# The first query and key projections of a four-layer kernel: paired 64-row matmuls, and a new order of loads, norms and output halves

## The chip, the cores and the metric

The kernel runs on one core of a Trainium2 chip. The metric is the device time of one execution in microseconds (us); the time before is 1153.98 us, the median of three runs (1153.71 to 1154.44).

## The reference

Four layers run in the order A, B, A, B on x of 2048 rows by 576 columns, each adding to x. Layer A is an attention over a dilated window:

```
qkv = layernorm(x) @ wqkv                 # 576 -> 3 * 576, 32 heads of 18
key of query s: s, s-2, ..., s-14         # 8 keys, those below 0 masked
x = x + softmax(q.k * 18**-0.5) v @ wo
```

Layer B is a gated MLP whose gate mixes over the rows:

```
z = gelu(layernorm(x) @ w_in)             # 576 -> 4608
g = w_sp @ layernorm(z[:, 2304:]) + b_sp  # over the 2048 rows
x = x + (z[:, :2304] * g) @ w_out
```

## The kernel before, in words

Nearly all of the time goes to layer B, whose matmuls run as pairs in 64-row halves of the array (`mm_phase`, L234): in a first phase output 0 takes the upper 64 rows and output 1 the lower 64, in a second phase they change places. A bank may take only one half at a time, so between the phases stands a token: a small ScalarE copy (`turn_on`) that waits for the end of the first phase and that the second phase waits for. The change concerns layer A, above all the first (li = 0), at the start of the program.

Layer A stores x with even rows first, then odd rows, so that a window is contiguous. The program order on every engine, SyncE's DMA queue (SP) among them, is the order of the code. The opening of layer 0 is written out by hand:

- The x tiles of 128 rows are loaded, `S_` takes their statistics on VectorE, `R_` their inverse deviation (GpSimd power, L728), `A_` normalizes them (L735). `T_pe` transposes tiles 0 to 3 on TensorE; `T_` (`ln_T`, L306) has the DMA transpose tiles 4 to 15 into `xnT`, from the SP queue.
- `VW(t, hh)` (L451) computes half of v of attention tile t, five matmuls 128x288, evicted to `v_ext`. Attention tile t covers 120 queries (the first 128), so VW(8) and VW(9) need normalized tile 8.
- `PG(d, qk, cc)` (L462) is a projection unit: 128 output columns (block d of 0 to 4) of q or k for the 512 rows of chunk cc, five matmuls of 128 contracted rows over 512 columns, the fifth (`wqk4`, columns 512 to 575) padded with zero rows. Its eviction (L445 on ScalarE, L443 on VectorE) goes to a staging tile `stg`. Once q and k of a block are complete for cc 0 and 1, eight DMAs, dealt to the POOL and SP queues, move the heads' rows into `QK`. Block 4 holds the rests of both q and k.
- The window's mask is 14 rows more of `QK` in each head's 32. They are built in `R` (rows[0] to rows[3]), written in 16-byte pieces to the DRAM tile `win_period` (rows[2]; its first columns by rows[3]), loaded back four times by `load_pat` into `win_pat`, and spread over `QK` by `fill_window_rows` (L201, L204) before the heads' rows are laid over them.

Before the change the order on TensorE is: `T_pe` with VW(0) to VW(3); 18 units, nine for cc = 0 and nine for cc = 1; VW(4) to VW(7); four units of cc = 2; the logits of step 0 (`L_mm`, L536); four more units of cc = 2; VW(8); then 34 steps. On SP: the loads, rows[2], the load of x tiles 12 to 15, `T_` of tiles 4 to 7, `load_pat`, `T_` of tiles 8 to 11, 17 DMAs to `QK`, `T_` of tiles 12 to 15.

Step s runs the logits of step s+1, their exponentials on ScalarE (L545), the product with v (`PV`, L559), and what a table adds: the remaining units (steps 0 to 9 for cc = 2 and 3), the remaining VW, halves of the output projection (`WO`, L629), and TensorE's transposes of attention output (`O_T`, L595) of the tiles in `pe_turn`. `units` says in which steps the 32 WO halves stand; those at 34 and later run behind the last step. The logits take three PSUM banks (X) and one of two (Y) in turn; the rest shares the other Y and three PT banks.

Of the kernel before, what the change touches and what calls it, by code (L numbers as in the profile page):

```python
# [12 lines left out]
f32 = mybir.dt.float32  # L13
# [50 lines left out]
class K:  # L64
# [53 lines left out]
    def build_window_rows(self, c, R):  # L118
# [30 lines left out]
        one = self.dram.tile([2, MR, 2 * P + 8], bf16, name="win_period")  # L149
        for xb in self.xn_bufs:  # L150
            nc.gpsimd.memset(xb[:, D:640], 0.0)

# [43 lines left out]

    def fill_window_rows(self, QK, half):
        nc, n = self.nc, self.cfg.S // 2
        for g0 in (0, 4):
            for a in range(2):  # L200
                nc.vector.tensor_copy(out=QK[:, a, g0:g0 + 4, half * n:(half + 1) * n].rearrange("p g (k x) -> p g k x", x=P),  # L201
                                      in_=self.pat[:, a, half, None, None, :].to_broadcast([P, 4, n // P, P]))
            if half == 0:
                nc.vector.tensor_copy(out=QK[:, :, g0:g0 + 4, 0:8], in_=self.pat0[:, :, None, :].to_broadcast([P, 2, 4, 8]))  # L204
# [132 lines left out]
    def zero_right(self, wqk=True):  # L337
# [4 lines left out]
        nc.vector.memset(R["wo"][64:128, 4, :], 0.0)  # L342

    def load_wqk(self, eng, twice=False):

        R = self.right
        for c0, n, w0 in ((D, 512, D + 64), (0, D, 0), (D + 512, 64, D)):
            self.dma(R["wqk"][:, :, w0:w0 + n], self.A_wqkv[0:512, c0:c0 + n].rearrange("(c p) n -> p c n", p=P), eng=eng)
            for r in ((0, 64) if twice else (0,)):
                self.dma(R["wqk4"][r:r + 64, w0:w0 + n], self.A_wqkv[512:576, c0:c0 + n], eng=eng)  # L350
# [30 lines left out]
    def layer_A(self, li):  # L381
# [206 lines left out]

        pe_turn = tuple(range(0, 6)) + tuple(range(7, NT - 2, 2)) + (NT - 3,) if li == 0 else ()

# [85 lines left out]
        if li == 0:  # L676
# [10 lines left out]
            x_load(x0[:, 0:1, :], 0, 1, nc.sync)  # L687
            x_load(x0[:, 1:2, :], 1, 1, nc.scalar)
            x_load(x0[:, 2:4, :], 2, 2, nc.sync)
            self.load_wv(nc.sync, 2)  # L690
# [3 lines left out]
            exp_table()  # L694
            self.zero_right()
            self.make_ident()
            warm = self.PT_tile([P, 512], f32, "warm")
            for _ in range(46):
# [3 lines left out]
                sb, oT[:].rearrange("p a b -> p (a b)")[:, 4 * D:4 * D + nR].rearrange("p (a r b m) -> p a r b m", a=2, r=MR, b=2))  # L702
            nc.scalar.copy(out=v_ext[:, :, :, DH:DH + 1], in_=self.ones[:, None, None, :].to_broadcast([P, NT, H, 1]))
            rows[0]()
# [26 lines left out]
            def A_(*tiles):  # L731
                for i in tiles:
                    xns[i] = xn = self.xn_bufs[self.xn_rr % len(self.xn_bufs)]
                    self.xn_rr += 1
                    nc.vector.tensor_scalar(out=xn[:, 0:D], in0=xts[i], scalar1=mvs[:, i, 0:1],  # L735
                                            scalar2=rstds[:, i:i + 1], op0=ALU.subtract, op1=ALU.mult)

            def T_pe(i):
# [8 lines left out]
            def T_(*tiles):  # L747
                for i in tiles:
                    self.ln_T(xns.pop(i), i * P, P)
# [10 lines left out]
            rows[2](nc.sync)  # L760
            A_(3)
            VW(2, 0, False)
            T_pe(3)
# [6 lines left out]
            S_(4, 5)  # L770
            R_(4, 2)
            A_(4, 5)
            T_(4, 5)
            S_(6, 7)
            R_(6, 2)
            rows[3](nc.gpsimd)
            A_(6, 7)
            T_(6, 7)
            S_(8)
            self.load_pat(nc.sync)  # L780
            S_(9, 10, 11)
            R_(8, 4)
            S_(12)
            A_(8, 9, 10, 11)
            T_(8, 9, 10, 11)
            self.fill_window_rows(QK, 0)
            S_(13, 14, 15)
            order = [(d, cc) for cc in range(2) for d in range(5)]
            for k_, (d, cc) in enumerate(order):
                for qk in ((1, 0) if d < 4 else (0,)):  # L790
                    PG(d, qk, cc, False, (nc.gpsimd, nc.sync) if d in (0, 3, 4) else q2)
                if k_ == 7:
                    R_(12, 4)
            nvw0, nvw = 4, 9
        else:
# [33 lines left out]
        def at(s, f, *a):  # L829
            table.setdefault(s, []).append((f, a))  # L830
# [10 lines left out]
        for k_, (d, qk, cc) in enumerate(pgs):  # L841
            at(k_ if li == 0 else (k_ * PG_END) // len(pgs), PG, d, qk, cc, True, *((q2,) if li == 0 else ()))
        vws = [(t, hh) for t in range(nvw, NT) for hh in range(2)]
        lag, twice = (PG_END - 5, (PG_END - 2,)) if li == 0 else (9, ())
        vsteps = ([x for x in range(PG_END - 4, NST - 3) if x % 4] if li == 0 else
                  [6, 6] + list(range(8, NST)))
        for k_, (t, hh) in enumerate(vws):
            assert vsteps[k_] <= 2 * t - 2 + hh
            at(vsteps[k_], VW, t, hh, (k_ % 2 == 0 or k_ > len(vws) - 4) if li == 0 else vsteps[k_] >= PG_END - 4 and k_ % 2 == 0)
        units = [x for x in range(lag, NST) for _ in range(2 if x in twice else 1)]  # L850
        units += [NST] * 3 + [NST + 1] * 2 + [NST + 2] * 2 if li > 0 else [NST] * 2 + [NST + 1] * 4
        wo_steps = list(zip(units[0::2], units[1::2]))
# [416 lines left out]
```

## Time and profile before

| what | value |
|---|---|
| profiled execution | 1153.91 us |
| its span, first to last instruction | 1152.1 us |
| mean granted TensorE clock | 1.000 |
| TensorE (matmul) busy | 1144.3 us, 12949 instructions |
| VectorE, ScalarE, GpSimd busy | 537.9, 371.8, 259.9 us |
| moved by DMA | 91.26 MB |

The span is cut by stage: the opening of layer 0 until about 48 us, its steps until 122 us, layer B until 581 us, the second layer A until 689 us, the second layer B until the end. A line of the timeline gives start, duration, engine, line, operation, out<-in and count, and in brackets the idle time before it and who ended it. A line of the chain of waits gives start, duration, engine, tile, line and count. "SPq" is the issuing of a DMA, not its transfer. Durations of matmuls in the timeline overlap; the chain's do not.

### The profile page before, as it was taken

What the parts mean: (1) busy time and instruction counts of PE and PEld (TensorE: products, weight loads), DVE (VectorE), ACT (ScalarE), POOL (GpSimd) and SP (SyncE); (2) the same over time, 40 slices, a digit from 0 to 9 for tenths busy, and PEclk for the clock granted to TensorE, in tenths of its full rate; (3) what the DMA queues carried; (4) which work ended last, traced back from release to release, by engine and by line L of the source; (5) the groups of instructions that cost most, each with busy time, mean ns of one, the idle gap of its engine ahead of it and who ended that gap; (6) DMA issues with size and microseconds to landing.
All of it is one profiled execution on the core that took longest, in us unless ns stands there. A gap on an engine that the chain in (4) does not pass through costs nothing.

```text
span 1152.1 us, 29708 instructions
## 1 busy us (share of the span) xinstructions
PE 1144.3 (99%) x12949; PEld 612.9 (53%) x12949; DVE 537.9 (47%) x1193; ACT 371.8 (32%) x665; POOL 259.9 (23%) x387
## 2 busy tenths in 40 slices
PE   9999999999999999999999999999999999999998
PEld 5567554444444444457755774544444444444676
DVE  8789887312233222234466889843322223222311
ACT  5589565011111111102247876641111111011000
POOL 3689654000000000002153767530000000000000
PEclk9999999999999999999999999999999999999999
DMA  8878597000000000049455777930000000000322
GB/s 194 182 166 197 135 201 152 13 13 13 13 1 13 13 13 2 1 143 221 109 111 112 172 161 167 227 83 1 13 13 13 13 13 1 13 1 28 103 74 58
DMA packets 177373, 91.26 MB, mean 79 GB/s; under 512 B 128788, under 2 KB 170420, under 8 KB 177242
## 3 DMA queue, kind: packets, MB, share of 16 engines
q1 hardware_dynamic: 164762, 70.75, 28.1%
q0 software_dynamic: 5888, 12.72, 4.5%
q10 hardware_dynamic: 6592, 5.90, 1.7%
q8 instruction: 101, 1.65, 0.6%
q14 instruction: 30, 0.25, 0.1%
HBM read 35.46 MB, written 14.69 MB: 44 GB/s over the span
## 4 chain that ended last, share of the span: by engine, by line
PE 97%; ACT 1%; DVE 1%; issue 1%; DVEq 0%; ACTq 0%
PE hh L234 79%; PE pp L462 6%; PE pv L451 3%; PE pw L629 3%; PE O_ps L559 2%; PE L_ps L536 2%; ACT P_sb L545 1%; PE L_ps L462 1%; PE hh L1191 0%; DVE ln_st L715 0%; PE pt L595 0%; DVE ln_xn L735 0%; ACT v_ext L445 0%; DVE win_bits L158 0%; ACT xnT L745 0%
## 5 line engine op out<-in xcount | busy, mean ns | idle before, releaser
L234 PE MATMUL hh<-Wq,Z 64*128 64x512 bf16 x4608 | 505.8, 376 | 0.0
L234 PEld LDWEIGHTS <-Z 64*128 64x128 bf16 x6984 | 338.3, 94 | 311.6
L1095 DVE TENSOR_TENSOR g_tmp<-hh,ln_xn 128x512 f32<-128x512 f32 x144 | 92.8, 686 | 452.3 <-PE hh L234 452.3
L947 ACT COPY bank_turn<-ones 1x1 bf16<-1x1 bf16 x239 | 44.7, 187 | 538.6 <-PE hh L234 538.6
L78 POOL DMA_DIRECT2D wout<-in_B_w_out_dram x4 | 4.3, 1075 | 602.0 <-PE hh L234 602.0
L234 PE MATMUL hh<-wout,Z 64*128 64x288 bf16 x2232 | 137.0, 283 | 0.0
L545 ACT ACTIVATE P_sb<-L_ps 128x1440 bf16<-128x1440 f32 (+3 forms) x136 | 125.1, 972 | 22.4 <-PE L_ps L536 21.1
L234 PE MATMUL hh<-xnT,w 64*128 64x512 bf16 x1152 | 132.1, 376 | 0.0
L234 PE MATMUL hh<-win2a,xnT 64*128 64x512 bf16 (+1 forms) x960 | 118.6, 355 | 0.0
L234 PEld LDWEIGHTS <-xnT 64*128 64x128 bf16 x1440 | 69.6, 94 | 70.3 <-issue 0.5
L1020 DVE BATCH_NORM_STATS2 z_st<-zp 128x6 f32<-128x512 bf16 (+1 forms) x160 | 92.6, 623 | 11.1 <-ACT zp L1018 11.1
L1086 ACT ACTIVATE z1T<-hh 128x1024 bf16<-128x1024 f32 x72 | 73.7, 1024 | 61.9 <-PE hh L234 61.9
L1096 DVE TENSOR_TENSOR Z<-g_tmp,z1T 128x512 bf16<-128x512 f32 x144 | 92.4, 683 | 0.0
L234 PEld LDWEIGHTS <-w 64*128 64x128 bf16 x1152 | 55.8, 94 | 68.5
L1018 ACT ACTIVATE zp<-hh 128x1024 bf16<-128x1024 f32 (+1 forms) x96 | 76.1, 810 | 48.8 <-PE hh L234 48.7
L462 PE MATMUL pp<-xnT,wqk_sb 128*128 128x512 bf16 (+1 forms) x330 | 75.5, 379 | 0.0
L234 PE MATMUL hh<-win2b,xnT 64*128 64x512 bf16 (+1 forms) x480 | 72.8, 355 | 0.0
L1160 DVE TENSOR_TENSOR x_new<-hh,xo 128x288 bf16<-128x288 f32 x64 | 26.3, 453 | 93.0 <-PE hh L234 89.3
L299 POOL TENSOR_SCALAR ln_xn<-x_new,ln_mv,ln_rstd 128x576 bf16<-128x576 bf16 x28 | 64.2, 2293 | 2.6
L78 POOL DMA_DIRECT2D QK<-stg x76 | 48.0, 635 | 36.2 <-DVE stg L443 22.0
L1044 POOL TENSOR_SCALAR Z<-zp,z_mv,z_rstd 128x256 bf16<-128x256 bf16 x32 | 51.2, 1599 | 3.5
L462 PEld LDWEIGHTS <-wqk_sb 128*128 128x128 bf16 (+1 forms) x360 | 32.1, 97 | 36.6 <-issue 2.3
(124 smaller groups left out, 754.1 us busy)
## 6 DMA issues: line engine op xcount, KB each, us to landing
xres<-x_new SPq DMA_DIRECT2D x44, 144.0 KB
wout<-in_B_w_out_dram POOLq DMA_DIRECT2D x4, 1296.0 KB, 7.6
xo<-xres SPq DMA_DIRECT2D x32, 144.0 KB
xn_rows<-ln_xn SPq DMA_DIRECT2D x28, 160.0 KB
w<-in_B_w_in_dram SPq DMA_DIRECT2D x16, 256.0 KB
QK<-stg POOLq DMA_DIRECT2D x51, 72.0 KB, 4.3
QK<-stg SPq DMA_DIRECT2D x37, 72.0 KB
xo<-in_A_x_dram SPq DMA_DIRECT2D x6, 288.0 KB
```

Of the source, the lines that this page charges most:

```text
L78: return eng.dma_start(out=out, in_=in_)
L234: ins = self.nc.tensor.matmul(outs[a_], lhsT=lhs(a_, c, r0), rhs=rhs(a_, c, r0), start=start and k_ == 0, stop=stop and k_ == len(chunks) ...
L299: e.tensor_scalar(out=xn[:nrows, 0:D], in0=x_t[:nrows, :], scalar1=mv[:nrows, 0:1], scalar2=rstd[:nrows, 0:1], op0=ALU.subtract, op1=ALU.mult)
L462: nc.tensor.matmul(pp, lhsT=w, rhs=self.xnT[r0:r1, c, cc * 512:(cc + 1) * 512], start=start, stop=stop, tile_position=(r0, 0))
L545: nc.scalar.activation(out=P_bufs[2 * jp + s % 2][:nk, :, :, 0:nq], in_=Lv[:nk, :, :, 0:nq], func=ACT.Exp, scale=scale)
L947: self.turn_on = lambda tok: nc.scalar.copy(out=tok, in_=self.ones[0:1, 0:1])
L1018: nc.scalar.activation(out=zp[:, w0:w0 + n], in_=pz, func=ACT.Gelu_apprx_tanh)
L1020: nc.vector.bn_stats(out=st[:, x // 512, :], in_=zp[:, x:x + min(512, w0 + n - x)])
L1044: eng.tensor_scalar(out=Z[:, b0:b1, i, :], in0=zv[:, b0:b1, :], scalar1=mv[:, 0:1], scalar2=rstd[:, 0:1], op0=ALU.subtract, op1=ALU.mult)
L1086: lambda ht, z1T=z1T, q2=q2: nc.scalar.activation(out=z1T[:, q2 * 512:(q2 + 2) * 512], in_=ht[:].rearrange("p a b -> p (a b)"), func=ACT.G ...
L1095: nc.vector.tensor_tensor(out=tmp[:], in0=pg[:, a_, :], in1=bsp[:, qs], op=ALU.add)
L1096: nc.vector.tensor_tensor(out=uT(jj)[:, sub, qs], in0=tmp[:], in1=z1Ts[jj, sub][:, qs], op=ALU.mult)
```

## The change

- The 18 units of cc 0 and 1 become nine pairs in 64-row halves (`PG_first` and its `second`), four chunks in the first phase, five in the second. The banks rotate over three pairs: two of X, the two of Y, two of PT. A pair's first phase stands ahead of the second phase of the pair before. The order is k and q of blocks 0 to 3 for cc = 0 (four pairs), then k with q of each block for cc = 1, then block 4. VW(4) stands around the second phase of the fourth pair, VW(5) around that of the last.
- `wqk4` and columns 576 to 639 of the normalized tiles hold the data of columns 512 to 575 twice, for tiles 0 to 7 by a GpSimd copy per tile, for the weights by three loads on the ScalarE queue (`load_wqk4_again`). The doubled weights are zeroed (VectorE) behind the last pair; the zeroing ahead of the opening and four GpSimd memsets go.
- rows[3] moves ahead, to the SP queue; `load_pat` moves from behind `T_` of tiles 6 and 7 to between `T_(4)` and `T_(5)`; the window fill is split in two among the norms. `T_` of tiles 8 and 9 stands behind the SP DMAs of block 0, that of tiles 10 and 11 behind those of block 1. `v_ext`'s ones are set by a GpSimd memset, not a ScalarE copy.
- VW(9) moves from steps 10 and 11 to ahead of the steps, and the VW behind it are dealt anew, so that steps 10 and 14 have none. VW evictions of the second layer A go to VectorE in other places. In both layers A one WO half moves from step 33 to step 32 (and in the second, halves at 34 to 36 to 33 to 35); tile 6 joins `pe_turn` in layer 0.

```diff
-        for xb in self.xn_bufs:
-            nc.gpsimd.memset(xb[:, D:640], 0.0)
...
+    def load_wqk4_again(self, eng):
+        for c0, n, w0 in self.WQK_PARTS:
+            self.dma(self.right["wqk4"][64:128, w0:w0 + n], self.A_wqkv[512:576, c0:c0 + n], eng=eng)
...
-        pe_turn = tuple(range(0, 6)) + tuple(range(7, NT - 2, 2)) + (NT - 3,) if li == 0 else ()
+        pe_turn = tuple(range(0, 7)) + tuple(range(7, NT - 2, 2)) + (NT - 3,) if li == 0 else ()
...
+            self.load_wqk4_again(nc.scalar)
...
-            self.zero_right()
+            self.zero_right(False)
...
-            nc.scalar.copy(out=v_ext[:, :, :, DH:DH + 1], in_=self.ones[:, None, None, :].to_broadcast([P, NT, H, 1]))
...
+                    if i < 8:
+                        nc.gpsimd.tensor_copy(out=xn[:, D:640], in_=xn[:, 512:D])
...
+            rows[3](nc.sync)
+            nc.gpsimd.memset(v_ext[:, :, :, DH:DH + 1], 1.0)
...
+            S_(6)
             A_(4, 5)
-            T_(4, 5)
-            S_(6, 7)
+            T_(4)
+            self.load_pat(nc.sync)
+            T_(5)
+            S_(7)
             R_(6, 2)
-            rows[3](nc.gpsimd)
+            S_(8)
             A_(6, 7)
             T_(6, 7)
-            S_(8)
-            self.load_pat(nc.sync)
+            self.fill_window_rows(QK, 0, (0,))
             S_(9, 10, 11)
             R_(8, 4)
             S_(12)
             A_(8, 9, 10, 11)
-            T_(8, 9, 10, 11)
-            self.fill_window_rows(QK, 0)
+            self.fill_window_rows(QK, 0, (4,))
             S_(13, 14, 15)
-            order = [(d, cc) for cc in range(2) for d in range(5)]
-            for k_, (d, cc) in enumerate(order):
-                for qk in ((1, 0) if d < 4 else (0,)):
-                    PG(d, qk, cc, False, (nc.gpsimd, nc.sync) if d in (0, 3, 4) else q2)
-                if k_ == 7:
-                    R_(12, 4)
-            nvw0, nvw = 4, 9
+            def PG_first(units, outs):
...
+                turn = self.mm_phase(outs, lhs, rhs, [0, 1, 2, 3], 0, True, False)
+                def second():
+                    self.mm_phase(outs, lhs, rhs, [0, 1, 2, 3, 4], 1, False, True, turn)
+                    for u, o in zip(units, outs):
+                        PG(*u, False, (nc.gpsimd, nc.sync) if u[0] in (0, 3, 4) else q2, pp=o)
+                return second
...
+            order = [((d, qk, 0), (d + 1, qk, 0)) for qk in (1, 0) for d in (0, 2)]
+            order += [((d, 1, 1), (d, 0, 1)) for d in range(4)] + [((4, 0, 0), (4, 0, 1))]
+            second = None
+            for p, units in enumerate(order):
+                if p == 4:
+                    self.ring = ["PT"]
+                    VW(4, 0, False)
+                    second()
+                    VW(4, 1, False)
+                    second = None
+                then = PG_first(units, pair_banks(p))
+                if second is not None:
+                    second()
+                    if p in (5, 6):
+                        T_(2 * p - 2, 2 * p - 1)
+                second = then
+            self.ring = ["Y", "Y", "PT", "PT", "PT"]
+            R_(12, 4)
+            VW(5, 0, True)
+            second()
+            nc.vector.memset(wqk4[64:128, :], 0.0)
+            VW(5, 1, False)
+            nvw0, nvw = 6, 10
...
-        lag, twice = (PG_END - 5, (PG_END - 2,)) if li == 0 else (9, ())
-        vsteps = ([x for x in range(PG_END - 4, NST - 3) if x % 4] if li == 0 else
+        lag, twice = (PG_END - 5, (PG_END - 2, NST - 2)) if li == 0 else (9, (NST - 2,))
+        vsteps = ([x for x in range(PG_END - 3, NST - 3) if x % 4 and x != PG_END] if li == 0 else
...
-            at(vsteps[k_], VW, t, hh, (k_ % 2 == 0 or k_ > len(vws) - 4) if li == 0 else vsteps[k_] >= PG_END - 4 and k_ % 2 == 0)
-        units = [x for x in range(lag, NST) for _ in range(2 if x in twice else 1)]
-        units += [NST] * 3 + [NST + 1] * 2 + [NST + 2] * 2 if li > 0 else [NST] * 2 + [NST + 1] * 4
+            at(vsteps[k_], VW, t, hh, k_ % 2 == 0 or (k_ > len(vws) - 4 if li == 0 else k_ < 6))
+        units = [x for x in range(lag, NST - 1) for _ in range(2 if x in twice else 1)]
+        units += [NST - 1] * (26 - len(units)) + [NST] * 2 + [NST + 1] * 4
```

More of the change, by code (lines that the diff above doesn't have):

```diff
@@ L195, in make_ident, with fill_window_rows @@
                                 base=0, pattern=[[-1, P]], channel_multiplier=1)
-    def fill_window_rows(self, QK, half):
+    def fill_window_rows(self, QK, half, g0s=(0, 4)):
         nc, n = self.nc, self.cfg.S // 2
-        for g0 in (0, 4):
+        for g0 in g0s:
             for a in range(2):
@@ L342, in zero_right @@
         nc.vector.memset(R["wo"][64:128, 4, :], 0.0)
+    WQK_PARTS = ((D, 512, D + 64), (0, D, 0), (D + 512, 64, D))
+    def load_wqk4_again(self, eng):
+        for c0, n, w0 in self.WQK_PARTS:
+            self.dma(self.right["wqk4"][64:128, w0:w0 + n], self.A_wqkv[512:576, c0:c0 + n], eng=eng)
     def load_wqk(self, eng, twice=False):
         R = self.right
-        for c0, n, w0 in ((D, 512, D + 64), (0, D, 0), (D + 512, 64, D)):
+        for c0, n, w0 in self.WQK_PARTS:
             self.dma(R["wqk"][:, :, w0:w0 + n], self.A_wqkv[0:512, c0:c0 + n].rearrange("(c p) n -> p c n", p=P), eng=eng)
@@ L794, in layer_A, with lhs, rhs @@
-            nvw0, nvw = 4, 9
+            self.turn_on = lambda tok: nc.scalar.copy(out=tok, in_=self.ones[0:1, 0:1])
+            def PG_first(units, outs):
+                def lhs(a_, c, r0):
+                    d, qk, cc = units[a_]
+                    w0 = d * P + (640 if qk else 0)
+                    return wqk[r0:r0 + 64, c, w0:w0 + P] if c < 4 else wqk4[r0:r0 + 64, w0:w0 + P]
+                def rhs(a_, c, r0):
+                    cc = units[a_][2]
+                    return self.xnT[r0:r0 + 64, c, cc * 512:(cc + 1) * 512]
+                turn = self.mm_phase(outs, lhs, rhs, [0, 1, 2, 3], 0, True, False)
[4 more added lines that the diff above has]
+                return second
@@ new lines, in pair_banks @@
+            def pair_banks(p):
+                if p % 3 == 0:
+                    return [X0[:, k_, :] for k_ in range(2)]
+                self.ring = [("Y", "PT")[p % 3 - 1]]
+                return [self.PT_tile([P, 512], f32, "pp")[:, :] for _ in range(2)]
+            order = [((d, qk, 0), (d + 1, qk, 0)) for qk in (1, 0) for d in (0, 2)]
[14 more added lines that the diff above has]
+                second = then
```

## The prediction

> **What bounds the kernel now.** I read the page's busy times first, then the chain of waits in order of time, then the timelines of the stages that the change touches.
>
> ```profile
> PE 1144.3 (99%) x12949; PEld 612.9 (53%) x12949; DVE 537.9 (47%) x1193; ACT 371.8 (32%) x665; POOL 259.9 (23%) x387
> PE 97%; ACT 1%; DVE 1%; issue 1%; DVEq 0%; ACTq 0%
> ...
> 13.61 19.47 PE pp L462 x90
> 33.08 4.90 PE pv L451 x40
> 37.98 4.32 PE pp L462 x20
> 42.79 4.42 PE pp L462 x20
> 47.21 1.23 PE pv L451 x10
> ```
>
> TensorE is busy for 99% and makes 97% of the chain. In the opening the chain is one unbroken row of matmuls from 13.61 to 48.44: 18 units in 19.47 (1.08 each), eight VW in 4.90 (0.61 each), four units of chunk 2, the first logits, four units, VW(8). So whatever shortens TensorE's work there counts, and so does any wait that opens there. Step 0 begins at 48.4. From the first chunk-2 unit to there it is 48.44 - 37.98 = 10.5 us, of which nothing changes.
>
> **TensorE's own work in the opening.**
>
> ```profile
> L234 PE MATMUL hh<-Wq,Z 64*128 64x512 bf16 x4608 | 505.8, 376 | 0.0
> ...
> 584.97 0.54 PE L_ps L462 x3
> 585.50 3.99 PE pp L462 x21
> 589.50 2.59 PE L_ps L462 x12
> ```
>
> Layer B's pairs do 4608 matmuls 64x512 in 505.8 us, 0.110 each, so two at a time take 0.220. A new pair needs 4 + 5 of these couples, 1.98 us, against 2.16 for two units: 0.18 saved, 1.7 over nine pairs. Against it: the array changes between 128-row and 64-row work. The second layer A shows that: from 584.97 to 589.50, 4.53 us, stand 8 half and 16 whole matmuls, worth 4 x 0.220 + 16 x 0.216 = 4.34; two changes cost 0.19, 0.1 each. The new opening has eight (into the pairs, in and out of each VW(4) half, in and out of VW(5), out at the end): 0.8. Net gain of the pairs: 0.9. Tokens and evictions (two of 0.59 and a copy per 1.98 us of ScalarE, a row below) stay hidden, since a second phase begins only behind the first phase of the next pair.
>
> VW(9) comes in addition, 1.2 us. Without any wait the first chunk-2 unit would begin at 37.98 - 0.9 + 1.2 = 38.3. VW(4) and VW(5) only change places.
>
> **The queue that feeds it.** Chunk cc = 1 needs tiles 4 to 7 transposed, chunk cc = 2 tiles 8 to 11; all of this goes through SP.
>
> ```profile
> 10.09 1.84 SPq L78 DMA_DIRECT2D win_period<-oT  x2
> 13.95 7.00 SPq L306 DMA_TRANSPOSE xnT<-ln_xn  x4
> 22.53 1.61 SPq L78 DMA_DIRECT2D win_pat<-win_period  x4
> 24.23 5.16 SPq L306 DMA_TRANSPOSE xnT<-ln_xn  x4
> 29.50 7.73 SPq L78 DMA_DIRECT2D QK<-stg  x9
> 37.33 6.41 SPq L78 DMA_DIRECT2D QK<-win2a  x8
> 43.85 5.19 SPq L306 DMA_TRANSPOSE xnT<-ln_xn  x4
> ...
> 17.91 0.76 POOL L78 DMA_DIRECT2D win_period<-win_first  x1 [0.31 <-POOL win_first L182]
> ...
> 25.42 2.36 DVE L201 COPY QK<-win_pat 128x4096 bf16<-128x4096 bf16 x2 [1.07 <-DMA win_pat<-win_period]
> ...
> 12.00:14.00 2.00, 1.81 (x14) 1.29 (x14) 1.12 (x5) 1.22 (x4) 0.70 (x1) 1.00 1.15 290
> 14.00:16.00 2.00, 2.00 (x11) 0.88 (x9) 1.92 (x7) 0.83 (x3) 0.00 (x0) 1.00 1.06 132
> 16.00:18.00 2.00, 2.00 (x11) 0.90 (x10) 1.17 (x4) 1.01 (x3) 1.36 (x6) 1.00 0.61 54
> 18.00:20.00 2.00, 2.00 (x11) 0.94 (x10) 1.93 (x8) 1.14 (x2) 0.66 (x1) 1.00 1.14 283
> ```
>
> Before, tiles 4 to 7 are issued by 20.95 and nine units from 13.61 reach cc = 1 at 23.35 without a pause: they landed within 2.4 us. `load_pat` stood behind them and waited until 22.53, 3.9 us after GpSimd's issue of rows[3] ended at 18.67. Now it stands ahead of T_(5), and all of SP waits with it for the period's 16-byte rows to land in DRAM.
>
> When do they land? They are issued at 10.09 to 11.93, but the windows show a queue that is full: 290 GB/s until 14, then 132 and 54 while the share of busy DMA stays at 1.06 and 0.61, then 283 again. A full queue that moves little is one of tiny pieces: I read the hole from 14 to 18 as these rows, behind the loads issued earlier. Floor: reached at 14 and landed 1.3 later (the lag of `load_pat` itself, issued until 24.14, used at 25.42), 15.3. Ceiling: the hole's end and 1.3, 19.3. The three extra weight loads (64 partitions x 1152 columns, 147 KB at 290 GB/s) push it 0.5 later. I take 18.1, near the end of the hole. Then four loads (1.61) end at 19.8, T_(5) to T_(7) (5.16 / 4 = 1.29 each) at 23.7, and land 1.4 later, at **25.1**; the lag is that of the plain load, and below the 2.4 of before.
>
> TensorE would want them at 13.61 + 4 pairs (7.9) + VW(4) (1.2) + five changes (0.5) = 23.2. It waits 1.9. This wait also swallows whatever moves ahead of it: the memset of the doubled weights and ScalarE's ones for `v_ext` that go, GpSimd's copy behind each normalized tile that comes.
>
> ```profile
> 1.10 0.54 DVE wqk_sb L340
> 2.59 2.54 ACT L703 COPY v_ext<-ones 128x544 bf16<-128x544 bf16 x1
> 17.00 0.78 DVE L735 TENSOR_SCALAR ln_xn<-x_in,lnx_mv,lnx_rstd 128x576 bf16<-128x576 bf16 x2 [0.81 <-POOL lnx_rstd L728]
> 28.74 9.79 POOL L78 DMA_DIRECT2D QK<-stg  x15 [5.88 <-ACT stg L445]
> 4.93 0.58 POOL L728 TENSOR_TENSOR lnx_rstd<-lnx_rstd,neg_half 128x1 f32<-128x1 f32 x1 [0.26 <-DVE lnx_rstd L727]
> 24.48 0.59 ACT L445 CAST stg<-pp 128x512 bf16<-128x512 f32 x1 [0.53 <-PE pp L462]
> ```
>
> They are worth from -0.5 (the memset's 0.54 off the start of VectorE's chain, if x has landed by then, which no row shows) to +0.6 (a GpSimd operation of 0.58 at most ahead of the first transposes); I take 0, as the 1.9 covers both ends. The `v_ext` memset on GpSimd lies between 0.1 and 2.5 us in its idle time; were VW evictions held by it, the same 1.9 covers that. On VectorE the norms of tiles 6 and 7 (17.00) come behind the statistics of tile 8, those of tiles 8 to 11 behind half the fill; SP asks for them at 21 and 32.5, with 3 us of room. On GpSimd the power for tiles 12 to 15 stands behind 19 DMAs, not 15 (0.65 each), so at about 29.2 + 12.4 = 41.6; SP gets to these tiles at 48.5.
>
> Second wait: T_ of tiles 8 to 11, formerly issued at 24.23 to 29.39 while SP had nothing else, now stand behind the DMAs of blocks 0 and 1. Block 0 is complete when the second phase of pair 4 is evicted: 25.1 + 0.9 + 0.9 + 1.1 + 1.2 (two evictions of 0.59) = 29.2. SP then issues four DMAs, T_(8, 9), three DMAs, T_(10, 11). A `QK` DMA takes (7.73 + 6.41) / 17 = 0.83: 29.2 + 7 x 0.83 + 4 x 1.29 = 40.2. Landing: between 1.3 (the plain load) and 4.3 (the page's median for `QK<-stg` from GpSimd, whose transfers share these DMA engines); I take 2.0, as the queue holds three such DMAs then, not the 17 it held before: **42.2**. TensorE would be there at 25.1 + 5 pairs (9.9) + VW(5) to VW(8) (4.9) + three changes (0.3) = 40.2. It waits 2.0 more.
>
> ```profile
> QK<-stg POOLq DMA_DIRECT2D x51, 72.0 KB, 4.3
> ```
>
> Step 0 so begins at 42.2 + 10.5 = 52.7 instead of 48.4: **+4.3**. The rest of the queue about keeps up: ten more DMAs end at 48.5, and were ready for the logits of step 1 before within 48.4 - 43.7 = 4.6, so by 49.9 to 53.1; tiles 12 to 15 are issued by 53.7, land by 55.7, and are wanted by the first cc = 3 unit at about 55.5. The window fill, moved ahead by `load_pat`, gains nothing: blocks 0 to 2 are later than the fill anyway.
>
> **The steps and the ends.**
>
> ```profile
> 69.28 0.39 PE L536 MATMUL L_ps<-QK 32*128 32x120 bf16 x16
> 71.73 0.39 PE L536 MATMUL L_ps<-QK 32*128 32x120 bf16 x16
> 78.29 0.39 PE L536 MATMUL L_ps<-QK 32*128 32x120 bf16 x16
> 80.35 0.39 PE L536 MATMUL L_ps<-QK 32*128 32x120 bf16 x16
> 90.98 3.74 ACT L545 ACTIVATE P_sb<-L_ps 128x1440 bf16<-128x1440 f32 x4
> 116.86 0.72 PE L559 MATMUL O_ps<-v_ext,P_sb 128*128 128x19 bf16 x16 [0.43 <-ACT P_sb L545]
> ...
> 627.20 0.39 PE L536 MATMUL L_ps<-QK 32*128 32x120 bf16 x16 [0.21 <-ACT P_sb L545]
> 683.42 0.72 PE L559 MATMUL O_ps<-v_ext,P_sb 128*128 128x19 bf16 x16
> ```
>
> Step 10 takes 71.73 - 69.28 = 2.45, step 14 80.35 - 78.29 = 2.06. Without their VW (0.6), and with a transpose more in step 14, TensorE needs about 1.85 and 1.7, but two exponentials take ScalarE 3.74, so no step is under 1.87: -0.6 and -0.2. At the end of layer 0 TensorE waits 0.43 for the last exponential (116.86); a WO half fills it: -0.4. In the second layer A the same wait is short (the transpose before ends about 683.2): -0.2, and the evictions off ScalarE take away the 0.21 at 627.20: -0.2. Sum -1.6. No row bounds the new places of these halves from above; a late row of `oT` would take back at most the 0.6.
>
> **Sum:** +4.3 - 1.6 = **+2.7**. The profiled execution took 1153.91 us (span 1152.1 and 1.8 around it; the median is 1153.98): **1156.6**.
>
> **A rule against it.**
>
> ```profile
> 6.03 0.45 PE L742 MATMUL pt<-ident,ln_xn 128*128 128x128 bf16 x5 [0.62 <-DVE ln_xn L735]
> ```
>
> The granted clock is 1.00 in every window above, and TensorE's wait of 0.62 at 6.03 lies ahead of them. The Trainium skill ("TensorE: Matmul & The Clock Gate", HAM oscillation) wants no idle gap over about 3.4 us, or the clock halves; no run here shows such a gap. My waits of 1.9 and 2.0 stay under it, and by the rule the sum stands unless either grows to that.
>
> **Rivals.**
> - *The order of SP alone decides.* The rows land by 16.2, tiles 4 to 7 by 23.2, and only the second wait is left: block 0 complete at 27.3, T_(11) issued at 38.3 and landed at 40.3. The opening is 40.3 - 38.0 = 2.3 longer, the sum +0.7, 1154.6. For it: the hole's first half; against: 54 GB/s until 18.
> - *Not slower: both transfers are hidden.* The place is SP's issue. If beside an emptier queue a `QK` DMA issues in 0.6 instead of 0.83, and tiles 4 to 7 land by 23.2, tiles 8 to 11 land by about 38.7: opening +0.7, total -0.9, 1153.0; with the changes of mode free (-0.8) and the memset's 0.5 in front, 1151.7 or less. It decides from a landing at 38.3. Against: 17 DMAs in a row at 0.83.
> - *The tail of the queue is late too.* With the lag of 4.3 behind tiles 12 to 15, they land at 58.0, wanted at 55.5: +2.5, 1159.1.
> - *The clock halves in a wait that grew.* After each wait as much work as it was long runs at half speed: +1.9 and +2.0, 1160.5.
> - *The pairs don't run two at a time.* Then a pair takes 3.9 us, +17 and more: 1172. Layer B's 0.110 speaks against it.
>
> **How the numbers follow.** Forecast 0.50, with 18.1 moved between 17.3 and 18.9 and the lag between 1.4 and 3: 1155.2 to 1158.4. SP alone 0.17, hidden 0.19, tail 0.09, clock 0.04, no overlap 0.01. A measurement of this kernel can tell 0.2%, 2.3 us, from no change: 1151.7 to 1156.3. The forecast is above it for 0.34 of its 0.50; with tail, clock and no overlap that is slower 0.48. Hidden is faster for 0.09 and same for 0.10; with SP alone and the forecast's 0.16 same is 0.43. The range from 1153.0 to 1159.4 takes in the forecast, SP alone, the tail and the slower half of hidden.
>
> **What would show it.** In the changed profile: the first `win_pat` load on SP at about 18; a pause of TensorE near 23 and 25, and one near 40 and 42, each ended by a DMA to `xnT`; pairs of 1.98 in between; step 0 near 52.7; steps 10 and 14 at 1.87. If `win_pat` goes out by 16, or the chain shows no pause there, the forecast is wrong, and the time lies nearer 1153.

## The result and the profile after

The changed kernel takes **1167.74 us** (median of five runs, 1165.06 to 1169.67) against 1153.98, a ratio of 1.0118 with a 95% interval from 1.0106 to 1.0129. The prediction was 1156.6 with a range to 1159.4: the sign was right, the size was not. The profiled execution took 1169.67, the slowest of the five; its span is 1167.9, 15.8 more than before.

From the page after: busy time by engine, the clock of TensorE in 40 slices of 29 us, and the chain by engine.

```profile
PE 1147.9 (98%) x13009; PEld 616.8 (53%) x13026; DVE 541.2 (46%) x1197; ACT 368.7 (32%) x669; POOL 262.3 (22%) x391
...
PEclk9799999999999999999999999999999999999999
...
PE 95%; DMA 1%; ACT 1%; DVE 1%; issue 1%; SPq 0%; POOL 0%; DVEq 0%; ACTq 0%
```

TensorE was busy 3.6 us longer for the same products, the second slice shows a clock of 0.7, and DMA now has 1% of the chain. The chain of waits after, in order of time (start, duration, what):

```profile
12.10 6.52 DMA win_period<-win_first
...
21.25 1.21 SPq L304
22.50 1.28 SPq L304
23.88 2.61 DMA xnT<-ln_xn
26.63 4.67 PE pp L232 x26
...
43.50 0.91 SPq L304
44.51 7.66 DMA xnT<-ln_xn
52.22 0.61 PE pp L466
53.04 6.62 PE pp L466 x18
```

It leaves TensorE twice: for the 16-byte rows of the mask period (the last of them, `rows[3]`, landed at 18.62) and the transposes behind them, and for a transpose of chunk 2. The timeline of TensorE shows the size of both gaps in brackets, and the anchors by which the stages are cut, first after, then before:

```profile
26.63 4.67 PE L232 MATMUL pp<-xnT,wqk_sb 64*128 64x512 bf16 x26 [3.02 <-DMA xnT<-ln_xn]
52.22 0.61 PE L466 MATMUL pp<-xnT,wqk_sb 128*128 128x512 bf16 x1 [8.61 <-DMA xnT<-ln_xn]
65.57 0.40 PE L540 MATMUL L_ps<-QK 32*128 32x128 bf16 x16
...
704.73 0.82 PE L232 MATMUL hh<-win2a,xnT 64*128 64x512 bf16 x6
```

```profile
48.37 0.40 PE L536 MATMUL L_ps<-QK 32*128 32x128 bf16 x16
...
689.26 0.82 PE L234 MATMUL hh<-win2a,xnT 64*128 64x512 bf16 x6
```

The logits of step 1 start at 65.57 instead of 48.37: the opening is **17.2 longer** (predicted 4.3). Layer B takes 459.26 us in both chains and starts at 138.18 instead of 122.15, so layer 0's steps and its end are 17.2 - 16.0 = 1.2 shorter (predicted 1.2). From there to the second layer B it is 566.55 instead of 567.11, 0.6 shorter (predicted 0.4). All that went wrong lies in the opening, and its parts in this execution are: the two gaps, 3.0 + 8.6; slow matmuls behind them, 1.8 + 3.0 (26 in 4.67 where the run with filled gaps, below, takes 2.91; four units and a pause in 7.37 where 4.32 are due); VW(9) 1.2; what is left for the pairs and all else is -0.4.

SP's timeline (issuing alone) says why the gaps are longer than predicted:

```profile
18.78 2.42 SPq L78 DMA_DIRECT2D win_pat<-win_period  x4
21.25 3.85 SPq L304 DMA_TRANSPOSE xnT<-ln_xn  x3
32.43 3.46 SPq L78 DMA_DIRECT2D QK<-stg  x4
36.00 3.28 SPq L304 DMA_TRANSPOSE xnT<-ln_xn  x2
39.38 3.14 SPq L78 DMA_DIRECT2D QK<-stg  x3
42.62 3.40 SPq L304 DMA_TRANSPOSE xnT<-ln_xn  x2
```

And the windows (duration, then busy time and count of PE, PEld, DVE, ACT, POOL, then clock, DMA share, GB/s) say what the slow matmuls are:

```profile
27.50:28.00 0.50, 0.50 (x6) 0.26 (x4) 0.47 (x2) 0.19 (x1) 0.00 (x0) 0.51 0.00 0
31.00:32.00 1.00, 1.00 (x14) 0.49 (x10) 1.00 (x2) 0.67 (x2) 0.00 (x0) 1.00 0.00 0
46.00:48.00 2.00, 0.00 (x0) 0.00 (x0) 0.77 (x2) 0.00 (x0) 2.00 (x4) 1.00 1.35 77
48.00:50.00 2.00, 0.00 (x0) 0.00 (x0) 0.00 (x0) 0.00 (x0) 1.01 (x2) 0.50 1.13 157
56.00:58.00 2.00, 2.00 (x6) 0.76 (x5) 0.69 (x1) 0.00 (x0) 0.00 (x0) 0.50 0.76 152
```

The clock falls to a half behind either gap: from 27.5 to 30.9, and from 48.0, while TensorE is still idle, to 58.2.

### The profile page after: what moved, and what is told of

Its sections match the earlier page's. It is cut to its first block, busy times and chain, and to the rows that moved or that the text cites. A ratio compares the mean times of both kernels' runs of the same rounds, so it can differ in the third digit from the quotient of the medians.

```text
span 1167.9 us, 29850 instructions
## 1 busy us (share of the span) xinstructions
PE 1147.9 (98%) x13009; PEld 616.8 (53%) x13026; DVE 541.2 (46%) x1197; ACT 368.7 (32%) x669; POOL 262.3 (22%) x391
## 3 DMA queue, kind: packets, MB, share of 16 engines
q8 instruction: 102, 1.67, 0.6%
## 4 chain that ended last, share of the span: by engine, by line
PE 95%; DMA 1%; ACT 1%; DVE 1%; issue 1%; SPq 0%; POOL 0%; DVEq 0%; ACTq 0%
PE hh L232 78%; PE pp L466 4%; PE pw L633 3%; PE pv L455 3%; PE O_ps L563 2%; PE L_ps L540 2%; ACT P_sb L549 1%; DMA xnT<-ln_xn 1%; PE pp L232 1%; DMA win_period<-win_first 1%; PE L_ps L466 1%; PE hh L1242 0%; SPq L304 0%; DVE ln_st L719 0%; PE pt L599 0%
## 5 line engine op out<-in xcount | busy, mean ns | idle before, releaser
L1069 ACT ACTIVATE zp<-hh 128x1024 bf16<-128x1024 f32 (+1 forms) x96 | 76.1, 810 | 48.8 <-PE hh L232 48.6
L1211 DVE TENSOR_TENSOR x_new<-hh,xo 128x288 bf16<-128x288 f32 x64 | 26.3, 453 | 92.6 <-PE hh L232 83.9
L466 PE MATMUL pp<-xnT,wqk_sb 128*128 128x512 bf16 (+1 forms) x225 | 57.5, 393 | 9.5 <-DMA xnT<-ln_xn 8.6
L455 PE MATMUL pv<-wv_sb,xnT 128*128 128x288 bf16 x340 | 50.0, 285 | 1.0 <-ACT xnT L751 0.8
```

Of the source, the lines that this page charges most:

```text
L455: nc.tensor.matmul(pv[:nk, 0:288], lhsT=self.xnT[:, c, k0_(t):k0_(t) + nk], rhs=wv_sb[:, c, hh * 288:(hh + 1) * 288], start=(c == 0), stop ...
L466: nc.tensor.matmul(pp, lhsT=w, rhs=self.xnT[r0:r1, c, cc * 512:(cc + 1) * 512], start=start, stop=stop, tile_position=(r0, 0))
L1069: nc.scalar.activation(out=zp[:, w0:w0 + n], in_=pz, func=ACT.Gelu_apprx_tanh)
```

## The experiments

The theory (A): the order of the opening's queues cost the time, above all the transposes of tiles 8 to 11 behind transfers to `QK`, and the clock on top. Its rivals: (B) the transfers to `QK` are late in any order, since the pairs complete the blocks in quick succession; or the pairs themselves cost time.

**Fillers in the gaps.** Is the slow work a matter of the clock?

```diff
                     VW(4, 1, False)
+                    fillers(10)      # matmuls 128x512 into a bank nobody reads
...
+            fillers(36)
             A_(12, 13, 14, 15)
```

> The changed kernel with idle matmuls in its two waits: ten of 128x512 (2.2 us at full clock) behind VW(4), 36 (7.8 us) ahead of the first unit of chunk 2; they write a bank that nobody reads. Both fit into the waits of 3.0 and 8.6. Theory A's part on the clock: the clock stays full, 1.6 and 2.7 us of slow work go, the waits themselves stay: 1163.4, 1162 to 1164.5. Rival: the matmuls behind the waits are slow for another reason (data that land piece by piece): 1167 to 1168.5.

Measured 1164.23 (ratio 1.0090, interval 1.0076 to 1.0104). The chain with fillers:

```profile
23.87 2.16 PE warm L826 x10
26.02 2.91 PE pp L232 x26
...
49.71 4.49 PE pp L466 x20
```

The same 26 matmuls take 2.91 instead of 4.67, the four units 4.49 instead of 7.37, and the mean clock is 1.00. So by the medians 3.5 of the 13.8 us are the clock (in the profiled execution after, which is slower than the median, 4.8); the gaps, still there behind the fillers, make up the rest.

**The transposes late, in the kernel before.** Does it need the pairs?

```diff
-            T_(8, 9, 10, 11)
             self.fill_window_rows(QK, 0)
...
+                if k_ in (5, 6):
+                    T_(2 * k_ - 2, 2 * k_ - 1)
```

> The kernel before, with one thing moved: the transposes of tiles 8 and 9 behind SP's transfers of block 0, those of tiles 10 and 11 behind those of block 1. No pairs, no earlier mask loads. Theory A: block 0's four DMAs go out when the window fill lets them, 28.7 to 32.2, the transposes by 42 and land 6 later, as in the changed kernel, near 48, while TensorE is there at 38.0: a wait of 10, some 3 more at half clock: 1166.5, 1163 to 1168. If the late landing needs the pairs, which complete the blocks in quicker succession: a lag of 2, a wait of 4 to 6 and its clock: 1158 to 1161.5.

Measured 1163.10 (1.0076, 1.0061 to 1.0090). SP's timeline and TensorE's:

```profile
35.70 3.53 SPq L306 DMA_TRANSPOSE xnT<-ln_xn  x2
```

```profile
45.27 6.37 PE L462 MATMUL pp<-xnT,wqk_sb 128*128 128x512 bf16 x20 [7.59 <-DMA xnT<-ln_xn]
```

Issued by 39.23, landed at 45.27: a lag of 6.0, as after the change (issued by 46.02, used at 52.22, 6.2). The gap is 7.6, and 20 matmuls take 6.37. This one move costs 9.2 us in a kernel without pairs, two thirds of what the whole change lost.

**Half the transfers left out.** What does the transpose wait for in the queue?

```diff
+                    if li == 0 and cb == 0 and d < 2 and queues[dma_rr[0] % len(queues)] is nc.gpsimd:
+                        continue
                     self.dma(dst, src, eng=queues[dma_rr[0] % len(queues)])
```

> The changed kernel without GpSimd's share of the transfers of blocks 0 and 1 to QK (left out: those heads' rows of QK hold the mask fill, so the output is not the reference's); SP's share, its order and its transposes stay. In the changed kernel the last transpose, issued by 46.02, lands 6.2 later. If transfers of both queues share the DMA engines and the transposes wait for those of both: it lands by 48, a lag of 3.5 or less, the wait is 4 to 5 instead of 8.6, 1160 to 1163. If only what stands ahead in SP's own queue counts: lag 5 or more, 1165.5 or more.

Measured 1163.57 (1.0076, 1.0061 to 1.0092), but the four runs lie in two groups, 1161.35 and 1161.66, 1165.47 and 1165.52, so that the time alone fits either case. The profiled one is the slowest: its first gap, ahead of everything that was left out, is 3.31, with 26 matmuls in 5.73 behind it. What decides is the rows of SP and TensorE at the second gap:

```profile
42.69 3.25 SPq L304 DMA_TRANSPOSE xnT<-ln_xn  x2
```

```profile
49.32 6.18 PE L466 MATMUL pp<-xnT,wqk_sb 128*128 128x512 bf16 x20 [4.12 <-DMA xnT<-ln_xn]
```

SP issues the same seven transfers and four transposes in the same order, yet it is through with them in 12.0 instead of 13.6, the lag falls to 49.32 - 45.94 = 3.4 and the gap to 4.1. GpSimd's transfers delay SP's transposes. The Trainium skill says so ("DMA: Bandwidth & Descriptors", Issuing engines are not separate DMA queues): DMAs of all issuing engines run on the same 16 DMA engines and interleave.

**The transposes early again.** The first of a series that undoes the orders one by one.

```diff
             A_(8, 9, 10, 11)
+            T_(8, 9, 10, 11)
             self.fill_window_rows(QK, 0, (4,))
...
-                    if p in (5, 6):
-                        T_(2 * p - 2, 2 * p - 1)
```

> The changed kernel with the DMA transposes of tiles 8 to 11 asked for on SP right behind the normalizing of these tiles, ahead of all transfers to QK, as before the change; nothing else moves. Theory A (the order of the queue: transposes that stand behind and among the transfers to QK land late, and TensorE, idle for 8.6 us, then works at half clock): the wait of 8.61 us goes, and with it the slow stretch behind it (18 matmuls in 6.62 us where 18 x 0.216 = 3.9 are due, 2.7 lost). 1167.7 - 8.6 - 2.7 = 1156.4, 1155.5 to 1157.5; the first wait of 3.0 stays. Theory B (the transfers to QK themselves are too late, whoever goes first): the four transposes, put ahead, push the transfers back, the first logits wait instead, and at least half of the 11.3 us stays: 1162 or more.

Measured 1160.1 (1.0055, 1.0041 to 1.0069): 7.6 of the 11.3 come back, more than B allows, less than A says. Nor is all of the 7.6 sure to be the transposes': the first gap, which this edit doesn't touch, is 2.06 in this profile against 3.02 after the change and 3.31 in the run before, and here the clock stays full behind it. It varies from one execution to the next. GpSimd, VectorE and TensorE show a third wait, which the second had hidden:

```profile
44.94 1.05 POOL L732 TENSOR_TENSOR lnx_rstd<-lnx_rstd,neg_half 128x4 f32<-128x4 f32 x1
```

```profile
46.02 1.45 DVE L739 TENSOR_SCALAR ln_xn<-x_in,lnx_mv,lnx_rstd 128x576 bf16<-128x576 bf16 x4 [5.02 <-POOL lnx_rstd L732]
```

```profile
48.12 0.68 PE L540 MATMUL L_ps<-QK 32*128 32x128 bf16 x13 [2.53 <-DVE stg L447]
```

GpSimd's power for tiles 12 to 15 stands behind all its transfers and comes at 44.94; VectorE waits 5.0 in the norm that needs it, with the evictions of chunk 2 queued behind; TensorE waits 2.5 for an eviction, and the clock halves again at 47.9.

**And the power early.**

```diff
-            R_(12, 4)
...
+                    if p == 7:
+                        R_(12, 4)
```

> As the first experiment (transposes of tiles 8 to 11 ahead of all transfers), and GpSimd's power for tiles 12 to 15 behind the transfers of block 2, not behind those of all blocks; the mask loads stay ahead of the transpose of tile 5. In the first experiment VectorE waited 5.02 us for that power, with the evictions of the chunk 2 units queued behind it, TensorE 2.53 for the evictions, and some 3.3 us ran at half clock after that. Theory (the power's place in GpSimd's queue is a third wait, which the wait for the transposes hides in the changed kernel): 2.5 and 1.7 go, 1160.1 - 4.2 = 1155.9, 1155 to 1157; the first wait of 2 stays. Rival (the power only follows transfers that are late anyway, and the logits wait for them): no more than 1 goes, 1159 or more.

Measured 1160.0 (1.0052, 1.0038 to 1.0066): nothing came back, and my theory of a third wait that costs 4.2 fell. TensorE's timeline:

```profile
46.85 0.23 PE L540 MATMUL L_ps<-QK 32*128 32x128 bf16 x3 [1.40 <-DMA QK<-stg]
```

With the power early, the logits wait for the transfers to `QK`; the units behind them start at 47.7 against 48.8. So the transfers are late here, as the rival said. Why is in SP's timeline:

```profile
19.97 13.85 SPq L304 DMA_TRANSPOSE xnT<-ln_xn  x7
33.92 8.42 SPq L78 DMA_DIRECT2D QK<-stg  x9
```

Seven transposes of 1.3 each take 13.9: SP stood waiting for the norms of tiles 8 to 11, and its first transfer went out at 33.9, 4.4 later than before the change. VectorE shows the norms behind the first half of the fill, and what the fill waits for:

```profile
21.37 2.36 DVE L199 COPY QK<-win_pat 128x4096 bf16<-128x4096 bf16 x2 [2.92 <-DMA win_pat<-win_period]
...
28.10 1.45 DVE L739 TENSOR_SCALAR ln_xn<-oT,lnx_mv,lnx_rstd 128x576 bf16<-128x576 bf16 x4 [0.17 <-POOL lnx_rstd L732]
```

**The window fill late again.** In the changed kernel half of the fill stands ahead of these norms on VectorE, and it waits for the mask loads.

```diff
-            S_(8)
             A_(6, 7)
             T_(6, 7)
-            self.fill_window_rows(QK, 0, (0,))
+            S_(8)
...
             T_(8, 9, 10, 11)
-            self.fill_window_rows(QK, 0, (4,))
+            self.fill_window_rows(QK, 0)
```

> The old order of the opening's queues with the pairs and the new dealing, but the mask loads stand ahead of the transpose of tile 5 as in the changed kernel; the window fill stays whole and behind the norms of tiles 8 to 11. Against the run with transposes and power early (1160.0), only the place of the fill differs. Theory (the early fill makes the norms of tiles 8 to 11 and SP's transposes of them late, and so all transfers to QK): the norms are done by 24, the transposes issued by 30.3 instead of 33.8, the logits of step 0 wait for nothing; what stays is the first wait of 2 and up to 1.5 at half clock: 1156.5, 1155.5 to 1157.5. Rival (the first wait alone makes the transfers late): 1159 to 1160.5.

The fill isn't quite the only difference: the statistics of tile 8 go back behind the norms of tiles 6 and 7. That moves these norms by no more than 0.1 (17.58 here, 17.68 in the run before).

Measured 1155.51 (1.0014, 1.0005 to 1.0023), 4.5 less. SP and TensorE:

```profile
20.04 10.60 SPq L304 DMA_TRANSPOSE xnT<-ln_xn  x7
30.74 7.65 SPq L78 DMA_DIRECT2D QK<-stg  x9
```

```profile
25.94 2.98 PE L232 MATMUL pp<-xnT,wqk_sb 64*128 64x512 bf16 x26 [1.37 <-DMA xnT<-ln_xn]
```

The last norm of tiles 8 to 11 ends at 26.3 instead of 29.6, the seven transposes take 10.6, the transfers begin at 30.7, no logits wait. Only waits for tiles 4 to 7 are left, 1.1 ahead of VW(4) and this one of 1.4, and they don't slow the clock.

**The mask loads late too: the queues in the old order** (but for `rows[3]`, which stays on the SP queue, and the `v_ext` memset, which stays on GpSimd). To the kernel above:

```diff
             T_(4)
-            self.load_pat(nc.sync)
             T_(5)
...
             T_(6, 7)
             S_(8)
+            self.load_pat(nc.sync)
```

> The changed kernel with its pairs, VW(9) ahead of the steps and the new dealing, but the queues of the opening in the order of before: mask loads behind the transposes of tiles 6 and 7, the whole window fill behind the norms of tiles 8 to 11, their transposes right behind these norms, and GpSimd's power for tiles 12 to 15 behind the transfers of block 2, not behind all of them. Theory A (what cost time is the order of the queues: SP's transposes behind transfers, VectorE's fill ahead of norms, GpSimd's power behind 19 DMAs with VectorE's evictions queued behind the norm that needs it): no wait is left but the one ahead of VW(4), for tile 4, 0.2 to 1.0; the opening is 0.3 to 1.2 longer than before the change, the steps and ends 1.6 shorter: 1153.2, 1152.4 to 1154.2. Rival (the pairs complete all blocks within 8 us, so the transfers pile up whatever the order): a wait of 2 or more ahead of the logits of step 0, 1156 or more.

Measured 1153.94 (0.9998, 0.9989 to 1.0007), the time of before. The transfers behind the pairs are in time, and the pairs with the rest of the opening cost no more than the dealing of the steps gives (below). One gap is left, ahead of VW(4):

```profile
21.97 0.79 PE L455 MATMUL pv<-wv_sb,xnT 128*128 128x288 bf16 x5 [1.55 <-DMA xnT<-ln_xn]
```

**The mask loads late, but the fill early** (they go behind the transposes of tiles 6 and 7, the fill stays): once alone and once with the transposes early. These two ran before the three above, and their outcome led to them. The first edit is of both, the second is that of the first run of the series.

```diff
             T_(4)
-            self.load_pat(nc.sync)
             T_(5)
...
             T_(6, 7)
+            self.load_pat(nc.sync)
             self.fill_window_rows(QK, 0, (0,))
```

> The changed kernel with the loads of the mask period back behind the transposes of tiles 6 and 7, as before the change; tiles 8 to 11 stay behind the transfers of blocks 0 and 1. Theory A: tiles 5 to 7 land by about 22, TensorE wants them at 23.6, so the first wait (3.0) goes with the half clock behind it (27.8 to 30.9, 1.6 lost); all that follows is 4.6 earlier, the second wait keeps its length: 1163.1, 1162 to 1164. Rival: the window fill, now later, holds back the transfers of block 0 and with them the transposes of tiles 8 to 11, so that these still land near 52: 1166.5 to 1168.

> Both orders as before the change: the mask loads behind the transposes of tiles 6 and 7, the transposes of tiles 8 to 11 behind them and ahead of all transfers to QK; the pairs, VW(9) ahead of the steps and the new dealing stay. Theory A: both waits and both slow stretches go, the opening is 0.3 longer than before the change (pairs -0.9, VW(9) +1.2), the steps and ends 1.6 shorter: 1152.7, 1152.0 to 1153.5. Theory B, or a cost of the pairs that the waits hide so far: 1154.5 or more.

Measured 1161.05 (1.0061, 1.0046 to 1.0076) and 1161.33 (1.0065, 1.0052 to 1.0078). The first came out below its range, the second missed its 1152.7 by far. VectorE and TensorE in the first of them:

```profile
24.78 2.36 DVE L199 COPY QK<-win_pat 128x4096 bf16<-128x4096 bf16 x2 [5.95 <-DMA win_pat<-win_period]
```

```profile
38.99 7.20 PE L455 MATMUL pv<-wv_sb,xnT 128*128 128x288 bf16 x35 [5.01 <-DVE v_ext L447]
```

The fill now waits 6.0 for loads that come later, VectorE's norms and VW evictions behind it, and TensorE 5.0 for an eviction (5.95 and 4.94 in the second). I had moved the loads and not what waits for them.

**The dealing of the steps alone,** in the kernel before, with the changed kernel's `units`, `vsteps` and evictions, and

```diff
-        pe_turn = tuple(range(0, 6)) + tuple(range(7, NT - 2, 2)) + (NT - 3,) if li == 0 else ()
+        pe_turn = tuple(range(0, 7)) + tuple(range(7, NT - 2, 2)) + (NT - 3,) if li == 0 else ()
...
-            nvw0, nvw = 4, 9
+            nvw0, nvw = 4, 10
```

> The kernel before with the dealing of the steps alone: VW(9) ahead of the steps, the VW behind it and the WO halves dealt anew in both layers A, tile 6 transposed by TensorE; the opening's units, queues and orders are those of before. By the prediction's terms: VW(9) ahead of the steps +1.2, steps 10 and 14 -0.8, end of the layer -0.4, second layer A -0.4: 1153.6, 1153.0 to 1154.0. If the new places of the halves cost something by themselves (a row of attention output that comes late): 1154.3 or more; if more steps gain than the prediction counted: under 1152.8.

Measured 1153.29 (0.9994, 0.9985 to 1.0002): by its median 0.65 faster, where 0.4 was expected; the interval takes in no change.

**An attempt at more:** the old queues, the `v_ext` memset later, VW(3) in the place of VW(4).

```diff
-            nc.gpsimd.memset(v_ext[:, :, :, DH:DH + 1], 1.0)
...
-            VW(3, 0, False)
-            VW(3, 1, False)
...
             T_(6, 7)
+            nc.gpsimd.memset(v_ext[:, :, :, DH:DH + 1], 1.0)
...
-                    VW(4, 0, False)
+                    VW(3, 0, False)
                     second()
-                    VW(4, 1, False)
+                    VW(3, 1, False)
```

> The old order of the opening's queues with the pairs and the new dealing, as in the run before of that kind, and two changes: GpSimd's memset of v_ext stands behind the norms of tiles 6 and 7 instead of ahead of the power of tiles 4 and 5, and VW(3) takes the place of VW(4) around the fourth pair (VW(4) goes where VW(5) was), since VW(3) needs only tiles that TensorE transposes itself. In that run TensorE waited 1.55 us ahead of VW(4) for a DMA transpose. If that wait is what the pairs still lack against the steps' dealing alone: 1153.9 - 1.5 = 1152.4, 1151.8 to 1153.0, faster than the kernel before by 0.1%. If the pairs merely reach tiles 5 to 7 sooner and wait there: 1153.3 to 1154.

Measured 1154.61 (1.0006, 0.9997 to 1.0014), no gain. TensorE:

```profile
23.36 2.98 PE L232 MATMUL pp<-xnT,wqk_sb 64*128 64x512 bf16 x26 [1.43 <-DMA xnT<-ln_xn]
```

The gap of 1.55 is gone and one of 1.43 stands ahead of the fifth pair, for tiles 5 to 7, as the expectation's other case had it, with a time 0.6 above its range. Before the change TensorE came to cc = 1 at 23.35; here the transposes let it begin at 23.36. What the first four pairs save can't be had while these set the time. They begin at 14.84 here, 13.95 before, behind SP's 1.56 for `rows[3]`; whether the pairs would gain with that out of the way, no run shows.

**The ladder.** Each kernel has one part more of the change than the one above it:

| part added | median us | step |
|---|---|---|
| dealing of the steps alone | 1153.29 | |
| pairs and the rest of the opening, old queues | 1153.94 | +0.65 |
| mask loads ahead of `T_(5)` | 1155.51 | +1.6 |
| half of the fill ahead of the norms of 8 to 11 (and the statistics of tile 8) | 1160.01 | +4.5 |
| GpSimd's power behind all transfers | 1160.10 | +0.1 |
| transposes of 8 to 11 behind transfers: the changed kernel | 1167.74 | +7.6 |

By the intervals of these runs a step of less than about 1.5 isn't told from nothing: +0.65 and +0.1 aren't, and +1.6 barely is. The last step also holds what the first gap differed by.

## Why the prediction was wrong, by its steps

- **Bound:** right. Gaps and slow matmuls of TensorE in the opening came through to the end nearly whole (17.2 there, 15.8 at the end, with the gains of the steps between).
- **Pairs, 1.98 each:** right, and with it the rival "the pairs don't run two at a time" fell. 18 matmuls take 1.94 in the chain, nine couples. The four pairs, VW(4) and changes took 9.76 from 13.85, with 0.20 of waiting; 9.6 was predicted. The net gain of 0.9 isn't seen in any run: as the last rows show, the transposes of tiles 5 to 7 swallow what the first four save. "VW(4) and VW(5) only change places" missed that VW(4) now wants tile 4 earlier: in the run with the queues in the old order at 20.4, 1.55 before its transpose is there.
- **First wait, 1.9:** right in kind, and 1.4 to 3.3 in size. The mask loads went out at 18.78 (18.1 predicted) but took 2.42, not 1.61; the lag of 1.4 behind the last transpose held (25.10 to 26.5). The rows landed at 18.62, not by 16.2, and so the rival "the order of SP alone decides" fell. By the ladder the early loads alone cost 1.6.
- **Second wait, 2.0: the step that failed; it was 8.6.** The term that was mis-sized most is the lag of the transposes behind their issue: "I take 2.0, as the queue holds three such DMAs then" counted SP's DMAs in front and not GpSimd's beside them. The lag was 6.2; the runs show 6.0 without pairs and 3.4 without GpSimd's share. Block 0 was complete at 32.4 instead of 29.2 (the first wait ended 1.5 later, the slow clock took 1.8), and seven transfers with four transposes took 13.6 instead of 11.0 (12.0 without GpSimd's share). In sum the landing came at 52.2 instead of 42.2, while TensorE was there at 43.6 instead of 40.2: 8.6.
- **The fill, which "gains nothing":** it was counted as a gain that doesn't come. With the transposes early it is a loss of 4.5, which the second wait covers in the changed kernel. It holds the norms of tiles 8 to 11; SP asking for them "at 21 and 32.5, with 3 us of room" was true only because it asked so late.
- **GpSimd's power at 41.6:** it came at 45.8, and I looked only for SP, not for the evictions on VectorE behind the norm. Moving it alone gave back 0.1, which isn't told from nothing, since the transfers are no earlier.
- **The clock:** the rival was there with a chance of 0.04, since waits of 1.9 and 2.0 stay under the 3.4 of the Trainium skill ("TensorE: Matmul & The Clock Gate", HAM oscillation). "By the rule the sum stands unless either grows to that" holds for the 8.6, not for the first: a gap of 3.0 halved the clock, and one of 2.5 did in the run with the transposes early (more below). Here page and measurement differ, and the measurement decides. The rival's price, as much work as the wait was long, came from no row and was wrong as well: 1.8 behind 3.0, 3.0 behind 8.6.
- **Steps and ends, -1.6:** right: 1.2 and 0.6 in the trace; 1153.29 with VW(9)'s 1.2 in the run of the dealing alone.
- **The rival "not slower"** needed both transfers hidden, and fell with them; "the tail of the queue" had a lag of 4.3, nearer to the 6.2 that came, but behind tiles 12 to 15 instead of tiles 8 to 11.

## What to carry to other kernels

A transfer that the next stage needs goes ahead of the bulk in time, whichever queue the bulk is on: price its landing by all transfers in flight, not by those in front of it in its own queue. Where a DMA or a wait is moved on an in-order engine, write down what stands behind it there and who waits for that, also where a longer wait hides it now. And several new orders at once can cover each other: undo them one by one from the good end, not only from the bad one.

## What the runs showed of the hardware

- The clock of TensorE is decided in periods of 3.41 us that run on regardless of the kernel. In the changed kernel it changes at 27.51, 30.92, 47.99 and 58.23 (read from windows of a quarter us, as in the row of 27.50 above): 1, 5 and 3 times 3.41 apart, the third of them while TensorE is idle. The Trainium skill has this ("TensorE: Matmul & The Clock Gate", Part 1: The HAM clock gate, a free-running window of 3413 ns), and the trace agrees. The page speaks of an idle window before the clock halves; here one that was partly busy was enough. To see how busy, cut the windows along the periods (the second pair of numbers is PE's busy time and count): the changed kernel's period ahead of 27.51, the two of the run with the transposes early (phase from its changes at 47.94 and 51.35), and the one ahead of 47.96 of the run with the power early too.

```profile
24.10:27.51 3.41, 0.88 (x10) 0.50 (x12) 3.31 (x10) 0.21 (x1) 0.00 (x0) 1.00 0.40 78
```

```profile
24.05:27.46 3.41, 1.67 (x16) 0.94 (x18) 3.31 (x10) 0.57 (x3) 0.00 (x0) 1.00 0.24 48
44.53:47.94 3.41, 1.07 (x8) 0.30 (x6) 1.92 (x5) 0.00 (x0) 3.19 (x5) 1.00 0.75 123
```

```profile
44.55:47.96 3.41, 1.54 (x20) 0.65 (x19) 0.83 (x2) 0.19 (x1) 1.73 (x4) 1.00 0.70 126
```

  Busy times of 0.88, 1.07 and 1.54 of 3.41 cost the clock at the period's end, 1.67 did not: here the line lies near half a period. The other four traces in which the clock halves, cut the same way, agree: their periods with 0.00 to 1.09 of work lost it, those with 1.97 or more kept it. So 1.9 us of idle time can be enough if one period holds all of it, while the gap of 2.06, which two periods share (1.74 in the longer part), did not halve it. The half clock stays until the end of a period that was busy nearly throughout: in the changed kernel the one from 51.41 to 54.82, with TensorE idle until 52.22 and 2.39 of work, did not give it back, the next did; over the seven traces 2.42 or less did not, 3.21 or more did.
- A GpSimd memset held up VectorE. VectorE's timeline after, where GpSimd's memset of `v_ext` ran from 11.18 to 13.62, and that of the run with the memset later:

```profile
12.24 1.40 DVE L731 TENSOR_SCALAR lnx_rstd<-lnx_mv 128x2 f32<-128x2 f32 x1
12.32 1.33 DVE L719 BATCH_NORM_STATS2 ln_st<-x_in 128x6 f32<-128x288 bf16 x2
```

```profile
12.32 0.17 DVE L731 TENSOR_SCALAR lnx_rstd<-lnx_mv 128x2 f32<-128x2 f32 x1
12.40 0.81 DVE L719 BATCH_NORM_STATS2 ln_st<-x_in 128x6 f32<-128x288 bf16 x2
```

An operation of 0.17 and two of 0.81 together took 1.40 and 1.33, and end when the memset ends.
